# First-head copies on one queue, later beta gates and a layer norm in two streams, in a kernel whose order a list scheduler makes

## The chip, the cores and the metric

The kernel runs on one core of a Trainium2 chip. The metric is device time in microseconds (us) of one execution; each time of a kernel is a median of several runs; what is read from a trace (spans, waits, clock) is one profiled execution. Engines are named as the profile names them: PE is the matmul engine, PEld its weight load, DVE, ACT and POOL the vector, scalar and general engines, SP the sync engine, whose queue issues most DMAs. "SPq" and "ACTq" are those queues.

## The reference, cut

Two attention layers (32 heads of 20, four segments of 512 tokens with a compressive memory, a sigmoid gate on `beta`) alternate with two feed-forward layers (FFN), each behind a layer norm without parameters, on 2048 tokens of width 640:

```python
x = A_x
x = x + _A_ref(_layernorm(x), A_wq, A_wk, A_wv, A_wo, A_beta)
x = x + _B_ref(_layernorm(x), B_w1, B_w2)      # the "second layer norm" feeds this
x = x + _A_ref(_layernorm(x), A_wq, A_wk, A_wv, A_wo, A_beta)
x = x + _B_ref(_layernorm(x), B_w1, B_w2)
# in _A_ref, for segment s: softmax(q k^T * scale + mask) v, mixed by g = sigmoid(beta)
# with phi(q) M / (phi(q) z), where M and z sum phi(k) v and phi(k) of earlier segments
```

## The kernel before

The kernel is not written in the order in which it runs. Each piece of work is a Python generator, a *stream*, that yields operations with the tokens they wait for; a list scheduler with a small table of guessed costs picks, again and again, the operation that it believes can start first. The result is a fixed instruction order for each engine. So an edit to one stream may reorder the whole program.

```python
SWITCH_NS = 96.0      # the scheduler's guesses; none of them is emitted
COLS_LAG = 1500.0
SEM_NS = 60.0
...
# Sched.run: among the heads of all streams
key = (round(start + late), 0.5 if op.urgent else prio, self.rank[id(st[1])], n)
if best is None or key < best[0]:
    best = (key, st, end, start, k, op)
...
self.P.waits(e, waits)          # emit on engine e
self.free[e] = end              # the scheduler's belief of when e is free again
```

The scores of two head groups at once are made in five *rounds*. A round takes two score buffers. A third is lent during the first 20 rounds; after that there are only two, so the next round can't start before the exponentials of the last have emptied them. Matmuls come in three kinds: full (projections, FFN), row-tiled (scores, L1078), column-tiled (L1172 and the leftover FFN block, L1345).

```python
ROUNDS = (((0, 0, 0),), ((0, 1, 0), (0, 3, 384)), ((0, 2, 0), (1, 2, 256)),
          ((1, 0, 0),), ((1, 1, 0), (1, 3, 384)))
...
ready = sorted((s for s in SC if s.free), ...)
if len(ready) < 2 ...:          # a round takes two free score buffers
    return None, None
```

The four places that the change touches:

```python
# 1. beta gates, in consts(): when the stream may go on to the sigmoid of beta
tb = yield dma("sp", sem_("d_beta"), ...)
yield Need("stg", 0, 0, 0, 1)
te = yield act(32, lambda e: e.activation(gt[:, 0, :], beta_bc[:], ACT.Exp), [tb], psum=False)
# ... five small DVE operations, then omg and maskg

# 2. second layer norm: one stream that does both pairs of tiles in turn
def lnorm(s, x_tks, pool_, parts=1):
    n = 4 // parts
    for p0 in range(0, 4, n):
        ...   # stats of n tiles, rstd, then normalise and DMA-transpose pairs
def ln_b(a, s):
    xa = [[("xA", a, s, i, 0), ("xA", a, s, i, 1)] for i in range(NJ)]
    xt, xtk = yield from lnorm(s, xa, XNT_B, parts=2)
    S.set("hx", a, s, tks=[xt] + xtk)

# 3. proj_ln: the first norm of segment 3 is held back
if (a, s) == (0, 3):
    yield Need("sc",3,4,1)

# 4. first_heads: copies of the first q and k heads; z=0 by SP, z=1 by ACT
tk = yield dma(("sp", "act")[z], sem, 2048 * (rb - ra), ...,
               ev + sl.tks, issue=720.0, rate=200.0)
```

The softmax here doesn't subtract the row's maximum and nothing guards it: scores larger than these inputs give would overflow.

## Time and profile before

| | before |
|---|---|
| median of 4 runs | 570.1 us (568.55 to 570.87) |
| profiled span | 568.2 us |
| median that the prediction started from (3 of them) | 570.66 us |
| PE busy | 555.0 us, 98% |
| DVE, ACT busy | 409 us, 412 us |
| changes between kinds of matmul, from the instruction order | 394 |

PE is the bound. These are two lines of the page: PE's busy time with its share of the span and number of instructions, and the granted PE clock in 40 slices, in tenths.

```profile
PE 555.0 (98%) x5212; PEld 297.3 (52%) x5212; DVE 409.1 (72%) x1049; ACT 412.4 (73%) x527; POOL 192.1 (34%) x302
...
PEclk9999998999999999999999999999999999999999
```

A busy PE can hide slack, since matmuls overlap. I therefore also worked with the starts of the matmuls in the trace: between two of 320 columns lie 136 ns, between two of 512 columns 216 ns. The Trainium skill, "TensorEngine Tiling (Array Packing)", Key Properties, says that a change of tiling mode drains the engine; the trace agrees and gives the price, if from the step between two starts the streaming time of the first matmul is taken off: 96 ns from full to row-tiled, 91 to 101 ns back, 93 ns from full to column-tiled, 96 ns back.

The chain of waits, by engine, says the same: most of the span is PE's own work.

```profile
PE 80%; DVE 11%; DMA 5%; ACT 2%; SPq 1%; issue 1%; POOL 0%
```

From the starts of the matmuls I worked out *lost time*: for each pair of neighbouring matmuls, what their starts lie apart beyond the usual step for that pair of shapes (the 30th percentile in the kernel before, capped at 270 ns above streaming). Usual steps sum to 540.1 us before, lost time to 23.5 us (waits, half clock and all small delays).

The view of waits, limited to 89 to 103 us, says who waited for whom (us in total, times, longest):

```profile
PE ps L1345 <- DMA xnT<-xn_tok: 2.1, 1, 2.1
```

And the timeline of PE there (start, duration, operation, and in brackets the idle time before it):

```profile
92.19 0.72 PE L1172 MATMUL ps<-PT,v_aug 128*21 128x512 bf16 x16
92.91 0.40 PE L1078 MATMUL ps<-pad 20*128 20x384 bf16 x8
95.36 0.73 PE L1345 MATMUL ps<-xnT,w_r 128*32 128x256 bf16 x20 [2.05 <-DMA xnT<-xn_tok]
```

After the score round at 92.91 nothing was left but the leftover FFN block, and that waited for the transposed output of the second layer norm. In the trace's clock record a stretch at half clock follows, from 96.4 to 99.8 us.

### The profile page before, as it was taken

The page shows a single profiled execution, that of the slowest core. Times are in us where ns is not written, and L with a number is a line of the kernel's source. Part 1 is how long each engine was busy: PE and PEld are TensorE (multiplying, and loading weights), DVE is VectorE, ACT ScalarE, POOL GpSimd, SP SyncE. Part 2 cuts the span into 40 slices and gives each one's busy share as a digit, 9 for nine tenths or more (in the row PEclk, how much of TensorE's full clock was granted, in tenths as well). Part 3 has the DMA queues.
Part 4 walks back from the last instruction along what each step waited for, and adds up shares of the span by engine and source line. Part 5 has one row for each costly group of instructions (what it writes and reads, how often), then busy time and mean ns, then how long its engine had stood idle before and what let it go on. Part 6 is the DMA issues. An engine that isn't in the chain of part 4 may idle for free.

```text
span 568.2 us, 12813 instructions
## 1 busy us (share of the span) xinstructions
PE 555.0 (98%) x5212; PEld 297.3 (52%) x5212; DVE 409.1 (72%) x1049; ACT 412.4 (73%) x527; POOL 192.1 (34%) x302
## 2 busy tenths in 40 slices
PE   7999998999999999999999999999999999999998
PEld 6554553445554454655445545565545553665655
DVE  5957887888899888986688795599866875553202
ACT  5699878889879888887987687587876778313140
POOL 5336343333344343443334343044431433200000
PEclk9999998999999999999999999999999999999999
DMA  8685998735273415853377131771328420532101
GB/s 265 144 219 160 224 180 174 218 78 99 76 185 70 80 42 164 127 83 59 99 167 117 20 66 44 176 143 20 66 57 195 91 62 18 90 69 51 44 0 48
DMA packets 129980, 60.92 MB, mean 107 GB/s; under 512 B 108802, under 2 KB 119810, under 8 KB 129922
## 3 DMA queue, kind: packets, MB, share of 16 engines
q1 hardware_dynamic: 129504, 59.62, 47.4%
q8 instruction: 41, 0.67, 0.5%
q10 hardware_dynamic: 418, 0.49, 0.3%
q14 instruction: 17, 0.14, 0.1%
HBM read 20.57 MB, written 12.85 MB: 59 GB/s over the span
## 4 chain that ended last, share of the span: by engine, by line
PE 80%; DVE 11%; DMA 5%; ACT 2%; SPq 1%; issue 1%; POOL 0%
PE ps L601 52%; PE ps L598 11%; PE ps L1078 7%; PE ps L1172 5%; DMA otk<-otu 2%; PE ps L969 1%; DVE stats L609 1%; ACT PT L1140 1%; PE ps L1211 1%; DVE xn_tok L653 1%; PE ps L1021 1%; PE ps L1345 1%; DMA oT<-o_sb 1%; DVE otu L1182 1%; DMA pad<-scr 1%; DVE phs L936 1%
## 5 line engine op out<-in xcount | busy, mean ns | idle before, releaser
L1140 ACT ACTIVATE PT<-ps 128x1024 bf16<-128x1024 f32 x320 | 308.9, 1028 | 61.0 <-PE ps L1078 58.2
L1152 POOL TENSOR_SCALAR_AFFINE_SELECT PT<-PT 128x512 bf16<-128x512 bf16 x256 | 166.6, 668 | 271.7 <-ACT PT L1140 271.7
L601 PE MATMUL ps<-w_r,hT 128*128 128x320 bf16 x768 | 123.0, 299 | 0.0
L601 PE MATMUL ps<-xnT,w_r 128*128 128x512 bf16 x416 | 115.3, 383 | 0.0
L1294 DVE TENSOR_TENSOR x_sb<-x_sb,ps 128x320 bf16<-128x320 bf16 x128 | 60.6, 481 | 64.7 <-PE ps L601 63.7
L601 PEld LDWEIGHTS ps<-w_r,hT 128*128 128x128 bf16 x768 | 73.1, 98 | 32.3 <-issue 5.2
L1078 PE MATMUL ps<-pad 20*128 20x512 bf16 (+3 forms) x1024 | 63.6, 302 | 2.1 <-ACT PT L1140 1.0
L601 PEld LDWEIGHTS ps<-xnT,w_r 128*128 128x128 bf16 x416 | 39.5, 98 | 43.6 <-issue 4.8
L609 DVE BATCH_NORM_STATS2 stats<-x_sb 128x6 f32<-128x320 bf16 x124 | 55.2, 472 | 3.2 <-DMA x_sb<-in_A_x_dram 3.0
L1374 ACT ACTIVATE hT<-ps 128x512 bf16<-128x512 f32 x56 | 33.5, 599 | 22.2 <-PE ps L601 21.6
L601 PE MATMUL ps<-wo_r,oT 128*128 128x320 bf16 x256 | 46.8, 300 | 0.0
L1078 PEld LDWEIGHTS ps<-pad 20*128 20x128 bf16 x1024 | 17.9, 92 | 52.0 <-ACT PT L1140 24.7
L1182 DVE CAST otu<-ps 128x512 bf16<-128x512 f32 x47 | 32.3, 687 | 15.2 <-PE ps L1172 15.0
L1372 DVE TENSOR_SCALAR hT<-ps 128x512 bf16<-128x512 f32 x48 | 32.9, 685 | 12.3 <-PE ps L601 11.7
L1172 PE MATMUL ps<-PT,v_aug 128*21 128x128 bf16 (+3 forms) x896 | 40.5, 301 | 0.0
L598 PE MATMUL ps<-xnT,w_r 128*128 128x512 bf16 x104 | 39.9, 384 | 0.0
L625 POOL TENSOR_TENSOR rstd<-lnU,mhalf 128x2 f32<-128x2 f32 (+2 forms) x26 | 20.6, 791 | 47.2 <-DVE lnU L621 45.0
L601 PE MATMUL ps<-wv_r,xnT 128*128 128x320 bf16 x192 | 36.5, 299 | 0.0
L601 PE MATMUL ps<-xnT,wk_r 128*128 128x512 bf16 (+1 forms) x128 | 34.9, 366 | 0.0
L601 PE MATMUL ps<-xnT,wq_r 128*128 128x512 bf16 (+1 forms) x128 | 34.6, 366 | 0.0
L935 ACT ACTIVATE stg<-stg 128x512 bf16<-128x512 bf16 x50 | 31.6, 635 | 3.4 <-DVE rtmp L933 3.2
L653 DVE TENSOR_SCALAR xn_tok<-x_sb,mv,rstd 128x640 bf16<-128x640 bf16 x60 | 30.4, 536 | 3.9 <-POOL rstd L625 3.8
(108 smaller groups left out, 675.1 us busy)
## 6 DMA issues: line engine op xcount, KB each, us to landing
pad<-scr SPq DMA_DIRECT2D x124, 80.0 KB
scr<-stg SPq DMA_DIRECT2D x34, 256.0 KB, 2.7
out_dram<-x_sb SPq DMA_DIRECT2D x16, 160.0 KB, 1.8
w_r<-in_B_w_dram SPq DMA_DIRECT2D x10, 216.0 KB, 2.7
w_r<-in_B_w_dram SPq DMA_DIRECT2D x13, 160.0 KB, 2.7
x_sb<-in_A_x_dram SPq DMA_DIRECT2D x10, 160.0 KB, 3.0
scr<-w_r SPq DMA_DIRECT2D x5, 256.0 KB, 3.0
wv_r<-in_A_wv_dram SPq DMA_DIRECT2D x1, 800.0 KB, 9.3
```

Source lines behind the costliest of these rows:

```text
L598: bk, tk = yield pe(mm_ns(n), [(lambda e, bk, a=a, b=b: e.matmul(bk.ap[:, 0:n] if len(b.shape) == 2 else bk.ap[:, 0:n].rearrange("p (i n) ...
L601: tk = yield pe(mm_ns(n), [(lambda e, k=k, a=a, b=b, bk=bk: e.matmul(bk.ap[:, 0:n] if len(b.shape) == 2 else bk.ap[:, 0:n].rearrange("p (i ...
L609: tk = yield dve(320, 1, lambda e, c2=c2: e.bn_stats(stats6[:, t % 12, c2, :], x_sb[:, t, c2 * 320:(c2 + 1) * 320]), xt)
L653: nm = lambda e, bx, t, k: e.tensor_scalar(bx.ap[:, k * D:k * D + D], x_sb[:, t + k, :], mv[:, t + k, 0:1], rstd[:, t + k:t + k + 1], ALU. ...
L1078: fns.append([(lambda e, z=z, j=j, hh=hh, N=N, o=o, sl=sl, q=hh % 2: e.matmul(slot.ap[:, q, o:o + N], sl.ap[32 * hh:32 * hh + DH, z, 0, 12 ...
L1140: tx = yield act(1024, lambda e, dst=dst, src=src: e.activation(dst, src, ACT.Exp, scale=SCALE), sc + pw)
L1152: tm = yield pool(600.0, lambda e, reg=reg: e.affine_select(out=reg, in_=reg, pattern=[[0, 4], [1, 128]], compare_op=ALU.is_ge, fill=0.0, ...
L1172: fns.append((lambda e, OD, j=j, hh=hh: e.matmul(OD.ap[32 * hh:32 * hh + DH + 1, 128 * j:L], VAUG[vx(a, s)][:, j, 4 * g + hh, :], pt.ap[:, ...
L1182: te = yield evac(L, 1, lambda e: e.tensor_copy(dst, OD.ap), lambda e: e.activation(dst, OD.ap, ACT.Copy), [tk] + OTU[0].tks)
L1294: ta = yield dve(320, 1, lambda e: e.tensor_tensor(x_sb[:, t, 320 * hf:320 * hf + 320], x_sb[:, t, 320 * hf:320 * hf + 320], bk.ap[:, 0:32 ...
L1372: th = yield evac(512, 1, lambda e, dc=dc, bk=bk: e.tensor_scalar(hT[:, dc, :], bk.ap[:, :], 0.0, None, ALU.max), lambda e, dc=dc, bk=bk: ...
L1374: lambda e, dc=dc, bk=bk: e.activation(hT[:, dc, :], bk.ap[:, :], ACT.Relu), [tk] + HT.tks)
```

## The change

The intent as one reads it: let each half of the second norm go as soon as its tiles are ready, so that the wait just shown shrinks; free ACT's queue of DMA issues; take the wait for beta off the front of ACT.

```diff
-            yield Need("stg", 0, 0, 0, 1)
+            yield Need("ex", 0, 1)                       # beta gates
...
-        def lnorm(s, x_tks, pool_, parts=1):
+        def lnorm(s, x_tks, slot, p0=0, n=NJ, key=None):
...
-            if (a, s) == (0, 3):                          # norm of segment 3
-                yield Need("sc",3,4,1)
...
-                        tk = yield dma(("sp", "act")[z], sem, ...
+                        tk = yield dma("sp", sem, ...      # first heads
...
-        def ln_b(a, s):
-            xt, xtk = yield from lnorm(s, xa, XNT_B, parts=2)
-            S.set("hx", a, s, tks=[xt] + xtk)
+        def ln_b(p):
+            def f(a, s):
+                key = ("hslot", a, s)
+                slot = Acq(XNT_B) if p == 0 else Need(*key)
+                xt, xtk = yield from lnorm(s, xa, slot, 2 * p, 2, key)
+                S.set("hn", a, s, p, tks=xtk)
+                if p == 1:
+                    t0 = yield Need("hn", a, s, 0)
+                    S.set("hx", a, s, tks=[xt] + t0 + xtk)
+            return f
...
-        S.add(2, each(ln_b))
+        S.add(2, each(ln_b(0)))
+        S.add(2, each(ln_b(1)))
```

More of the change, by code (lines that the diff above doesn't have):

```diff
@@ L633, in turn @@
             return tk
-        def lnorm(s, x_tks, pool_, parts=1):
-            n = 4 // parts
+        def lnorm(s, x_tks, slot, p0=0, n=NJ, key=None):
             done = []
             xt = None
-            for p0 in range(0, 4, n):
+            if True:
                 aggr = []
@@ L649, in lnorm @@
                 if xt is None:
-                    xt = yield Acq(pool_)
+                    xt = yield slot
+                    xt = xt[0] if isinstance(xt, list) else xt
+                    if key is not None and p0 == 0:
+                        S.set(*key, tks=[xt])
                 for i in range(p0, p0 + n, 2):
@@ L744, in proj_ln @@
                 yield Need("sc",2,3,1)
-            if (a, s) == (0, 3):
-                yield Need("sc",3,4,1)
             early = a == 0 and s in (1, 2)
-            xt, xtk = yield from lnorm(s, xw, [XNT_E[s - 1]] if early else XNT_A)
+            xt, xtk = yield from lnorm(s, xw, Acq([XNT_E[s - 1]] if early else XNT_A))
             xt.users = []
@@ L885, in first_heads @@
                         p0 = 32 * hh + ra - r0
-                        tk = yield dma(("sp", "act")[z], sem, 2048 * (rb - ra), lambda e, p0=p0, ra=ra, rb=rb, c=c, z=z: e.dma_start(
+                        tk = yield dma("sp", sem, 2048 * (rb - ra), lambda e, p0=p0, ra=ra, rb=rb, c=c, z=z: e.dma_start(
                             sl.ap[p0:p0 + rb - ra, z], stg[ra - 128 * c:rb - 128 * c, c]), ev + sl.tks, issue=720.0, rate=200.0)
@@ L1326, in out_proj @@
             return f
-        def ln_b(a, s):
-            xa = [[("xA", a, s, i, 0), ("xA", a, s, i, 1)] for i in range(NJ)]
-            xt, xtk = yield from lnorm(s, xa, XNT_B, parts=2)
-            S.set("hx", a, s, tks=[xt] + xtk)
+        def ln_b(p):
+            def f(a, s):
+                xa = [[("xA", a, s, i, 0), ("xA", a, s, i, 1)] for i in range(NJ)]
+                key = ("hslot", a, s)
[6 more added lines that the diff above has]
+            return f
         HALF = {}
```

## The prediction

> **What bounds the kernel.** The median is 570.66 us, the profiled span 568.2 us. In the busy table PE has 555.0 us (98%), ACT 412, DVE 409, POOL 192. The chain of waits is 80% PE. Matmuls overlap, so busy PE can hide slack; their starts in the timeline don't: 136 ns apart for 320 columns and 216 ns for 512, nearly everywhere. Summing those steps over the 5212 matmuls (row- and column-tiled ones four abreast) gives about 505 us, my estimate of pure streaming. The rest is mostly changes between full, row-tiled and column-tiled matmuls, 0.1 to 0.26 us each in the timeline. The Trainium skill's "TensorEngine Tiling (Array Packing)", Key Properties, says a change of tiling mode drains the engine; the gaps agree.
>
> Real waits of PE are few: about 3.5 us before 10 us (first loads and norm), 0.5 at 21 us, 0.9 at 32 us (pad from scratch), 0.9 at 55 us, and the largest, 2.05 us at 93 us, where the first leftover FFN block waits for the second layer norm's transpose. A half-clock stretch follows, 96.4 to 99.8 us, costing up to 1.7 us (estimate: half of 3.4). Everything removable is about 8 us, 1.4%.
>
> **What the change does.** No arithmetic is added or removed, and the instruction order has 394 changes of tiling mode in both kernels. It is a rescheduling.
> 1. First heads: ACT's five issues (0.7 us each) go to the sync queue. ACT's 2.4 us gap at 15 us should shrink. The second head lands near 22.5 us (estimate); its first use is at 24 us. Near zero.
> 2. Beta gates leave the front of ACT and DVE and return later. Near zero.
> 3. Layer norm for segment 3 is no longer held back, and the second norm's halves have their own streams. Segment 1's projections move forward: the pause of the exponentials at 61 to 68 us disappears, and score rounds are a group of five ahead when the first leftover FFN block comes.
> 4. The cost: just before that block the new order has three successive score rounds with only 0.3 us of full matmuls among them. A round is gated by two exponentials of 0.97 us plus handovers, about 2.6 us. I estimate 8 us of rounds against 3.3 us of PE work, so the stall near 100 us grows from 2 to about 5 us, again followed by a half-clock stretch.
>
> So 2 to 3 us are gained early, about 3 us are lost at the first FFN, and the tail, dense FFN matmuls from about 475 us, is untouched. ACT's total is unchanged and bounds nothing.
>
> **Predicted:** 570.0 us, 564.5 to 575.5 at 8 in 10. Faster by over 2%: 0.02; within 2%: 0.95; slower: 0.03.
>
> **What would show each step.** Busy table: PE, ACT and DVE within 1% of before. Waits: PE's waits from 92 to 106 us total 4 to 6 us; those near 55 us shrink. Timeline: no 2.4 us gap of ACT at 15 us; no pause of the exponentials at 61 to 68 us; first scores still near 18 us. Granted clock: one half-rate stretch in mid-span.
>
> **What would make it wrong.** The small rounds overlap work I counted as serial, and the stall vanishes (then about 565). The fuller sync queue delays the scratch loads at 32 us, and each later round waits behind it. The reordering makes new waits in later segments, where today there are almost none.

## More of the kernel before

Where PE is short of work shows in this view of stretches: start and end, their length, then the busy time of each engine, PE's clock, the DMA share and GB/s.

```profile
core 0: us, PE busy (x) PEld busy (x) DVE busy (x) ACT busy (x) POOL busy (x), PEclk, DMA share, GB/s
15.00:50.00 35.00, 33.12 (x413) 17.88 (x411) 27.04 (x75) 29.52 (x38) 14.23 (x22) 1.00 0.72 178
50.00:75.00 25.00, 24.01 (x298) 13.53 (x295) 19.91 (x59) 21.74 (x30) 10.86 (x16) 1.00 0.88 211
75.00:90.00 15.00, 14.69 (x138) 7.17 (x137) 14.96 (x40) 13.09 (x18) 7.07 (x10) 1.00 0.76 141
90.00:106.00 16.00, 13.95 (x128) 5.35 (x127) 10.51 (x24) 12.67 (x18) 5.20 (x8) 0.89 0.85 181
106.00:300.00 194.00, 192.84 (x1864) 97.82 (x1863) 163.42 (x408) 166.12 (x204) 77.97 (x119) 1.00 0.51 110
```

In the stretch from 90 to 106 us PE is busy for 13.95 of 16 us, at a mean clock of 0.89.

## The result, and the profile after

The changed kernel took 573.68 us (median of 4, 573.09 to 573.99) against 570.1 us; the ratio is 1.0065, 95% interval 1.004 to 1.009. Ratios here compare the fast runs of the two kernels in the same rounds, so they are not quite the ratios of the medians, nor of the table's medians to 570.1.

Busy time and clock after:

```profile
PE 556.5 (97%) x5212; PEld 298.3 (52%) x5212; DVE 411.8 (72%) x1048; ACT 414.4 (72%) x528; POOL 192.2 (34%) x302
...
PEclk9999999899999999999999999999999999999999
```

The chain by engine has more of ACT in it (5%, before 2%), the first sign that exponentials now hold PE up:

```profile
PE 83%; ACT 5%; DMA 5%; DVE 5%; SPq 2%; issue 0%; POOL 0%
```

The matmuls are the same 5212. Usual steps sum to 540.4 us, nearly as before, lost time to 27.1 us: 3.6 us more, which is most of the 4.0 us between the spans. The stretches after, in the same columns:

```profile
15.00:50.00 35.00, 33.98 (x395) 18.16 (x393) 25.05 (x69) 30.07 (x40) 12.77 (x20) 1.00 0.75 183
50.00:75.00 25.00, 22.10 (x306) 11.88 (x303) 22.20 (x62) 23.55 (x29) 13.47 (x20) 1.00 0.94 202
75.00:90.00 15.00, 15.00 (x150) 7.87 (x147) 14.54 (x38) 13.18 (x18) 6.62 (x10) 1.00 0.82 164
90.00:106.00 16.00, 12.51 (x142) 4.99 (x134) 13.16 (x35) 13.51 (x16) 7.27 (x12) 0.79 0.74 181
106.00:300.00 194.00, 191.68 (x1808) 96.52 (x1804) 159.76 (x398) 156.99 (x191) 74.28 (x113) 1.00 0.47 101
```

Two of the short ones lost: from 50 to 75 us PE is busy for 22.10 us instead of 24.01, and from 90 to 106 us for 12.51 instead of 13.95, at a clock of 0.79 instead of 0.89. The waits behind the first loss, in the changed kernel and then in the kernel before, from 50 to 75 us:

```profile
PE ps L1078 <- ACT PT L1140: 1.2, 2, 0.9
PE ps L1021 <- DMA phk<-phs: 0.9, 1, 0.9
PE ps L1211 <- POOL PT L1152: 0.3, 1, 0.3
PE ps L598 <- DMA hT<-xn_tok: 0.2, 1, 0.2
```

```profile
PE ps L598 <- DVE w_r L786: 0.9, 1, 0.9
```

(The last stretch, 106 to 300 us, is also 1.2 us less busy, but it holds fewer matmuls, 1808 instead of 1864, since the changed kernel does them at another time.) The waits of PE from 92 to 106 us:

```profile
PE ps L1078 <- ACT PT L1140: 3.4, 2, 2.0
```

The releaser is no longer the norm's transpose but the exponentials. The timeline of PE shows why:

```profile
94.94 0.40 PE L1078 MATMUL ps<-pad 20*128 20x384 bf16 x8
95.26 0.72 PE L1172 MATMUL ps<-PT,v_aug 128*21 128x512 bf16 x16
97.36 0.40 PE L1078 MATMUL ps<-pad 20*128 20x256 bf16 x8 [1.38 <-ACT PT L1140]
99.79 0.61 PE L1078 MATMUL ps<-pad 20*128 20x512 bf16 x4 [2.03 <-ACT PT L1140]
100.49 1.25 PE L1172 MATMUL ps<-PT,v_aug 128*21 128x512 bf16 x16
101.67 0.81 PE L969 MATMUL ps<-BD,phs 128*128 128x147 bf16 x6
102.43 0.61 PE L1078 MATMUL ps<-pad 20*128 20x384 bf16 x8
102.98 1.26 PE L1352 MATMUL ps<-xnT,w_r 128*32 128x256 bf16 x20
```

Four score rounds (L1078) stand at 94.94, 97.36, 99.79 and 102.43 us. Between the first three PE has only one column-tiled group; between the last two a group and six short matmuls (L969). Each round waits until two exponentials of the one before it, about 0.97 us each, have freed its buffers; the first three rounds start 2.42 and 2.43 us apart. I call a round *empty* when PE has next to no full matmuls (under about 0.9 us of them) between it and the next round. From 100.49 on matmuls take longer than usual: the column-tiled group 1.25 us instead of 0.72. The clock record has half clock from 98.2 to 105.0 us, twice as long as before. The leftover FFN block (L1352) comes at 102.98 us, with no wait of its own.

### The profile page after: what moved, and what is told of

Same layout as the page of the kernel before. It is cut to its first block, busy times and chain, and to the rows that moved or that the text cites. A ratio compares the mean times of both kernels' runs of the same rounds, so it can differ in the third digit from the quotient of the medians.

```text
span 572.2 us, 12815 instructions
## 1 busy us (share of the span) xinstructions
PE 556.5 (97%) x5212; PEld 298.3 (52%) x5212; DVE 411.8 (72%) x1048; ACT 414.4 (72%) x528; POOL 192.2 (34%) x302
## 4 chain that ended last, share of the span: by engine, by line
PE 83%; ACT 5%; DMA 5%; DVE 5%; SPq 2%; issue 0%; POOL 0%
PE ps L601 54%; PE ps L598 11%; PE ps L1078 8%; PE ps L1172 6%; ACT PT L1140 5%; DMA phk<-phs 2%; PE ps L969 2%; PE ps L1021 1%; DMA pad<-scr 1%; PE ps L1352 1%; DMA oT<-o_sb 1%; DVE stats L609 1%; SPq L906 1%; DMA x_sb<-in_A_x_dram 1%; DVE x_sb L1294 1%; SPq L631 0%
## 5 line engine op out<-in xcount | busy, mean ns | idle before, releaser
L1078 PE MATMUL ps<-pad 20*128 20x512 bf16 (+3 forms) x1024 | 63.8, 303 | 5.4 <-ACT PT L1140 4.6
L1381 ACT ACTIVATE hT<-ps 128x512 bf16<-128x512 f32 x58 | 34.7, 598 | 22.0 <-PE ps L601 21.5
L1078 PEld LDWEIGHTS ps<-pad 20*128 20x128 bf16 x1024 | 17.9, 92 | 55.5 <-ACT PT L1140 29.8
L1379 DVE TENSOR_SCALAR hT<-ps 128x512 bf16<-128x512 f32 x46 | 31.4, 683 | 9.6 <-PE ps L601 9.5
L787 ACT ACTIVATE stg<-ps 128x512 bf16<-128x512 f32 (+1 forms) x44 | 24.4, 560 | 13.4 <-PE ps L601 13.1
L936 DVE TENSOR_TENSOR phs<-stg,rtmp 128x512 bf16<-128x512 bf16 x50 | 23.5, 471 | 13.2 <-ACT stg L935 12.3
```

The costliest lines, as they stand in the source:

```text
L1078: fns.append([(lambda e, z=z, j=j, hh=hh, N=N, o=o, sl=sl, q=hh % 2: e.matmul(slot.ap[:, q, o:o + N], sl.ap[32 * hh:32 * hh + DH, z, 0, 12 ...
L1379: th = yield evac(512, 1, lambda e, dc=dc, bk=bk: e.tensor_scalar(hT[:, dc, :], bk.ap[:, :], 0.0, None, ALU.max), lambda e, dc=dc, bk=bk: ...
L1381: lambda e, dc=dc, bk=bk: e.activation(hT[:, dc, :], bk.ap[:, :], ACT.Relu), [tk] + HT.tks)
```

## The experiments

The parts were tried alone and one by one removed, and the instruction order of each build was compared first, with buffers and waits. Two findings needed no chip. With the beta edit undone, or with the segment 3 edit undone, or both, the changed kernel's program is *identical* on all five engines: once the copies are on the sync queue, these two edits decide nothing. And the copies' move alone gives the same program as all edits but the split norm. So the changed kernel is two edits: the copies, and the split. The empty rounds are already in the order of the copies' move alone.

The theory, A: the move of the copies leads the scheduler to an order with empty rounds, and these, with the half clock behind them, cost the time. Rivals: B, the split norm costs it; C, nine copies in line on the sync queue delay what stands behind them; D, the loss is spread over many places.

This table holds the lost time of one profiled execution by PE's progress (its sum of usual steps; 45 us of it are reached near 51 us of the span, 75 near 85, 95 near 108). "Half clock" is what its clock record shows between 10 us and the last 10 us; it can differ from run to run of one kernel (see "The idle rounds filled").

| run | median us | ratio to before | lost to 45 | 45 to 75 | 75 to 95 | after 95 | half clock us |
|---|---|---|---|---|---|---|---|
| before | 570.1 | 1 | 6.1 | 1.3 | 5.0 | 11.2 | 3.4 |
| changed | 573.68 | 1.0065 | 4.9 | 4.2 | 7.0 | 11.1 | 6.8 |
| heads_only | 576.03 | 1.0122 | 5.7 | 3.5 | 8.9 | 11.2 | 10.2 |
| ln_only | 570.73 | 1.002 | 5.6 | 2.9 | 0.8 | 15.4 | 6.8 |
| before_order_sync_issue | 571.83 | 1.0045 | 8.4 | 2.9 | 4.5 | 11.5 | 10.2 |
| after_order_act_issue | 572.95 | 1.0065 | 5.0 | 3.8 | 7.6 | 9.7 | 6.8 |
| after_switch_100 | 568.66 | 0.999 | 4.6 | 4.5 | 1.1 | 11.0 | 0 |
| after_sem_62 | 573.08 | 1.0075 | 4.6 | 3.5 | 7.3 | 10.5 | 6.8 |
| beta_only | 566.99 | 0.996 | 5.5 | 3.4 | 1.2 | 11.6 | 0 |
| beta_and_ln | 571.67 | 1.0036 | 5.4 | 3.6 | 2.7 | 13.8 | 0 |
| gate_only | 569.62 | 1.0005 | 5.6 | 1.3 | 5.3 | 10.9 | 3.4 |
| before_sem_62 | 575.02 | 1.0099 | 5.6 | 3.6 | 7.6 | 13.4 | 10.2 |
| beta_cols_1400 | 569.84 | 1.0005 | 5.0 | 3.7 | 2.6 | 13.0 | 0 |

One more run, after_filled, has matmuls added and stands by itself below.

### The copies alone

```diff
-  tk = yield dma(("sp", "act")[z], sem, ...     # in the kernel before
+  tk = yield dma("sp", sem, ...
```

> The kernel before with only the first heads' five copies moved to the sync queue. Its instruction order has the same three score rounds with almost no full matmuls (0, 0 and 0.5 us) that the changed kernel has. Theory A (the order that the move of the copies brings about costs the time): 1.005 to 1.009 of before, and waits of the tensor engine of 4 to 6 us between 92 and 106 us. Theory B (the two-stream layer norm costs it): 0.998 to 1.002.

Measured: 576.03 us, ratio 1.0122 (1.0102 to 1.0143), slower than expected. The largest of PE's waits from 92 to 106 us is the changed kernel's (3.8 us in all, below the 4 to 6 us expected):

```profile
PE ps L1078 <- ACT PT L1140: 3.4, 2, 2.0
```

The half-clock stretch is 10.2 us long, three times that of before. So the copies' move brings the loss; on top of it the split norm, which is all that sets the changed kernel apart from this one, gives back about half of it (1.0122 to 1.0065, each against before in its own rounds).

### The split norm alone

The edits to `lnorm` and `ln_b` of the diff above, nothing else.

> The kernel before with only the second layer norm as two streams. Theory A: 0.996 to 1.003 of before, since no run of empty rounds is in its order. Theory B: 1.005 to 1.009. If the split does what it is meant to, the 2 us wait at 93 us is shorter.

Measured: 570.73 us, ratio 1.002 (0.9999 to 1.0041): Theory B, that the split costs the time, falls. The split does what it is meant to. PE's waits from 89 to 103 us, then from 106 to 125 us:

```profile
PE ps L1080 <- ACT PT L1142: 0.2, 1, 0.2
```

```profile
PE ps L1080 <- ACT PT L1142: 1.6, 1, 1.6
```

The 2.05 us wait at 93 us is gone, and by 108 us of before's span this run is 3.1 us ahead in lost time. Then a wait for exponentials at 117 us takes 1.6 us, with a half-clock stretch behind it, and the rest goes in small waits later. The gain is real where it was aimed and is given back in another place.

### Order or queue: two crossed kernels

Here the scheduler plans as in one kernel while the five copies are emitted to the other kernel's queue:

```diff
-            self.P.waits(e, waits)
+            q = getattr(op, "put", e)
+            self.P.waits(q, waits)
...
-                tk = self.P.dma(e, fns[0][0], op.dma)
+                tk = self.P.dma(q, fns[0][0], op.dma)
...
-                        tk = yield dma(..., issue=720.0, rate=200.0)
+                        op = dma(..., issue=720.0, rate=200.0)
+                        op.put = "sp"                    # before's order, sync queue
+                        # or ("sp", "act")[z]            # changed order, both queues
+                        tk = yield op
```

> Every engine keeps the order of the kernel before; only the five copies of the first heads are really issued by the sync queue instead of ACT's. Theory A (order): within 1 us of before, 0.998 to 1.002. Theory C (nine copies in line on the sync queue delay the scratch loads and with them the scores): 1.004 or more, with longer waits of the scores for the pads near 32 us. ACT's 2.4 us gap at 15 us should be gone in either.

> Every engine keeps the order of the changed kernel; only the five copies are issued by ACT's queue again. Theory A (order): within 1 us of the changed kernel, 1.005 to 1.008 of before, with the waits between 95 and 104 us still there. Theory C: back to 0.998 to 1.002.

In the changed order the queue makes no difference: 572.95 us and 1.0065, the changed kernel's ratio. This agrees with the Trainium skill, "DMA: Bandwidth & Descriptors", Issuing engines are not separate DMA queues, which says that several issuing engines save only the sequencer's time to issue.

In before's order it costs: 571.83 us, 1.0045 (1.0023 to 1.0066), against the expectation of Theory A. This is Theory C in the form given above, though not through the scratch loads that its expectation named: no wait for them is left near 32 us (0.93 us in before). What is delayed is the beta load. ACT's timeline in before (one line), then in this run:

```profile
19.28 0.23 ACT L563 ACTIVATE gt<-beta_bc 128x32 f32<-128x32 bf16 x1 [1.22 <-DMA beta_bc<-in_A_beta_dram]
```

```profile
17.45 0.60 ACT L788 ACTIVATE stg<-ps 128x512 bf16<-128x512 f32 x1 [2.00 <-PE ps L602]
21.05 0.23 ACT L564 ACTIVATE gt<-beta_bc 128x32 f32<-128x32 bf16 x1 [3.00 <-DMA beta_bc<-in_A_beta_dram]
21.18 1.00 ACT L1143 ACTIVATE PT<-ps 128x1024 bf16<-128x1024 f32 x1
```

The beta load stands behind six copies on the sync queue instead of four and is issued at 18.39 us instead of 16.43. ACT, which works in order, waits 3.00 us for it (1.2 us in before) with the first exponentials standing behind, and PE then waits 1.9 us for these instead of 0.5. So the beta edit looks like the companion of the copies' move, but before's order with both was not run. (The profiled execution is the slowest of this kernel's six, 573.83 us, with more half clock than the others had, so its 10.2 us in the table is not typical.) In the changed kernel the scheduler knew the load was late and had put the gates back by itself, hence the edit without effect. ACT's 2 us of idleness at 15 us are there even without its issues (2.00 us before the operation at 17.45): it waited for a matmul group, not for its queue.

### The same edits, without the empty rounds

```diff
-SWITCH_NS = 96.0          # in the changed kernel; a guess of the scheduler
+SWITCH_NS = 100.0
```

```diff
-SEM_NS = 60.0             # in the changed kernel
+SEM_NS = 62.0
```

> The changed kernel with one number of the scheduler's own cost table altered (its guess of a mode change, 96 to 100 ns), which changes nothing but the order, from the 102nd row of the tensor engine on. No round with under 0.9 us of full matmuls is left ahead of the first leftover FFN block. Theory A (order, the empty rounds): waits between 92 and 106 us fall under 2 us, and the time falls by 3 to 5 us, to 0.998 to 1.002 of before. Rival D (the changed kernel loses time spread over many places, the empty rounds are only where it shows): 1.004 or more.

> The changed kernel with another number of the same table altered (handover, 60 to 62 ns). Its order is the changed kernel's through row 380 of the tensor engine, so the three empty rounds stay, and differs only later. Theory A: 1.004 to 1.010 of before. It also tells how much a different order after 130 us is worth: I expect 1.5 us at most.

The first has all the edits of the change but no empty round: 568.66 us, ratio 0.999 (0.9972 to 1.0008). Its waits of PE from 89 to 106 us and the stretch from 90 to 106 us:

```profile
PE ps L1078 <- ACT PT L1140: 0.2, 1, 0.2
```

```profile
90.00:106.00 16.00, 15.82 (x156) 6.99 (x155) 15.72 (x44) 14.16 (x19) 6.66 (x10) 1.00 0.97 208
```

PE is busy for 15.82 of 16 us at full clock. The second keeps the changed order past 104 us, empty rounds included, and differs only later: 573.08 us, 1.0075 (1.0052 to 1.0097). Two builds of the same edits, about 4.4 us apart, and of their lost time 6.2 us apart between 75 and 95 us of progress. Between these two builds Rival D, that the loss is spread out, falls.

Against before the account is less simple. Of the lost time that the changed kernel has more than before, 2.0 us stand between 75 and 95 us of progress, where the empty rounds are, but 2.9 us between 45 and 75, and 1.2 us were gained earlier. after_switch_100 pays the middle part as well (4.5 us) and makes it up where it has no empty rounds (1.1 us instead of before's 5.0). Theory A is thus shown for the stretch of the empty rounds; what costs the 2.9 us ahead of it was not tested.

### Empty rounds without any of the edits

```diff
-SEM_NS = 60.0             # in the kernel before
+SEM_NS = 62.0
```

> The kernel before, none of the four edits made, with the scheduler's handover guess set to 62 ns: a new order with two empty rounds ahead of the first leftover FFN block (before has none ahead of it). Theory A says the empty rounds cost whatever brought them about: 3 us or more of waits at 88 to 100 us, 1.002 to 1.006 of before. If empty rounds as such cost nothing, 0.998 to 1.001.

Measured: 575.02 us, 1.0099 (1.0067 to 1.0132), slower than expected. PE's timeline has the two empty rounds, at 94.37 and 96.91 us (the next round comes at 100.64):

```profile
94.37 0.40 PE L1078 MATMUL ps<-pad 20*128 20x384 bf16 x8
96.91 0.40 PE L1078 MATMUL ps<-pad 20*128 20x512 bf16 x4 [2.14 <-ACT PT L1140]
98.38 0.93 PE L1172 MATMUL ps<-PT,v_aug 128*21 128x512 bf16 x8 [1.08 <-POOL PT L1152]
```

Empty rounds cost here too, 7.6 us lost between 75 and 95 instead of 5.0. This build also has a 2.1 us wait at 54.5 us and more lost later than before has, so not all of its 1% is theirs. It is also a warning: a guess altered by 2 ns, and no work at all, moves this kernel by 1%.

### The idle rounds filled

```diff
+        def keep_warm():
+            for m, u, n in ((6, 1, 14), (6, 2, 26)):
+                t = yield Need("sc", m, u, 1)
+                bk, tk = yield pe(26.0, [(... e.matmul(bk.ap[:, 0:128], ident[:], ident[:], ...), k == n - 1)
+                                         for k in range(n)], t[1:], acq=MISC, mode="rows")
+                bk.release(tk)
...
+        S.add(1, keep_warm())         # in the changed kernel
```

> The changed kernel with 14 and 26 matmuls of the identity, whose results nobody reads, in the two long waits at 96 and 98 us; the order is otherwise the changed kernel's up to the first leftover FFN block, and differs a little after it. Theory A1 (the half clock after the waits comes from the idleness): no half-clock stretch near 98 to 105 us, and 1 to 2 us faster than the changed kernel. If the clock falls to half all the same, the idleness is not its cause. The waits for the exponentials are as long in either case, only filled.

The fillers and the rounds they stand between, on PE:

```profile
97.31 0.96 PE L591 MATMUL ps<-ident 128*128 128x128 bf16 x14
98.75 0.40 PE L1087 MATMUL ps<-pad 20*128 20x256 bf16 x8 [0.49 <-ACT PT L1149]
99.25 1.62 PE L591 MATMUL ps<-ident 128*128 128x128 bf16 x26
101.18 0.39 PE L1087 MATMUL ps<-pad 20*128 20x512 bf16 x4 [0.30 <-ACT PT L1149]
```

The clock record has no half-clock stretch left in this execution, and all four runs show a granted clock of 1.0 (the changed kernel's four: 0.994), so the idleness brings it about. The waits for exponentials shrink to 0.49 and 0.30 us because 0.96 and 1.62 us of useless matmuls stand in them.

From the round at 94.94 us to the sixth after it, at 111.13 us, the changed kernel takes 16.19 us; here it is 15.51 us, from 96.33 to 111.84 us. These 0.7 us are not the price of the half clock, since the work in the two stretches differs: the changed kernel's has the leftover FFN block and 16 full matmuls of 512 columns after the block, the filled one's has no block and 22. Over the first three rounds, where the useful work is the same, it is 7.49 against 7.28 us. The starts of the changed kernel's matmuls in its half-clock stretch add up to 2.6 us more than the usual steps (1.6 us in before's stretch); how much of that would have been waiting anyway is not known.

The recorded runs give another measure. Of the 33 runs of the kernel before that were made beside the experiments, 12 show a granted clock of 1.0 and 19 of 0.997 (one stretch of 3.4 us at half clock lowers the mean by 0.003), and their mean times are 568.56 and 569.66 us. So a stretch goes with about 1.1 us, though a run may be slower for the wait that brings the stretch as well.

The filled kernel as a whole was slower, 575.99 us (1.0118), where 1 to 2 us less than the changed kernel had been expected; the order after the FFN block differs and has new waits of up to 1.2 us between 188 and 205 us; as a version it is no use.

### The other edits alone, and tries at a faster version

```diff
-            yield Need("stg", 0, 0, 0, 1)      # beta_only, in the kernel before
+            yield Need("ex", 0, 1)
```

> The kernel before with only the beta gates moved behind the first score rounds (copies still split over two queues). In the changed kernel this edit alters no instruction, but alone it gives another order, without empty rounds, with the pause of the score rounds shortened. ACT no longer waits 1.2 us for beta ahead of the first exponential. Theory A: 0.994 to 1.000 of before.

Measured: 566.99 us (566.78 to 567.39), ratio 0.996 (0.9946 to 0.9974). The stretch from 90 to 106 us:

```profile
90.00:106.00 16.00, 15.81 (x156) 6.81 (x155) 12.84 (x38) 14.58 (x19) 6.67 (x10) 1.00 0.83 230
```

There is no empty round, no half clock, and 1.2 us lost between 75 and 95 us of progress where before has 5.0. It is the one version that is faster than the kernel before beyond the noise, by a little.

> The changed kernel with only the move of the five copies undone (they stay on two queues). Theory A: the move of the copies is what brings the empty rounds, so without it the stall near 97 us is gone and the time is 0.994 to 1.000 of before, about that of the beta edit alone. If the two-stream norm or the beta edit were to blame, it would stay at 1.004 or more.

The copies' move undone in the changed kernel: 571.67 us, 1.0036 (1.001 to 1.0061). This missed its expectation. The part that Theory A speaks of came true (2.7 us lost between 75 and 95, no half clock), but 13.8 us are lost later, against 11.2 in before, in waits of 0.7 to 0.9 us at 192, 241, 251 and 363 us among others. Theory A tells the loss of one stretch, not the total.

> The kernel before with only the layer norm of segment 3 no longer held back. In the changed kernel this edit alters no instruction; alone its order parts from before's at row 160 of the tensor engine, with one empty round ahead of the first leftover FFN block. Theory A: about like before, 0.998 to 1.004, with 2 to 3 us of waits at 88 to 98 us.

Segment 3's norm not held back, in the kernel before: 569.62 us, 1.0005, within its expectation, with the wait for exponentials at 92.5 us that its one empty round foretold.

> A try at a version faster than both: the beta edit alone, with another of the scheduler's guesses altered (the lag for column-tiled matmuls, 1500 to 1400), whose order has no empty round from the 20th round on. Theory A: 0.993 to 0.999 of before.

`COLS_LAG` at 1400 with the beta edit: 569.84 us, 1.0005 (0.9974 to 1.0035). Missed: 2.6 us lost between 75 and 95, but 13.0 later. An order without empty rounds does not by itself make a good time.

## Why the prediction was right or wrong

The range (564.5 to 575.5) and the class (within 2%) held. The central figure, 570.0, was 3.7 us too low: a gain of 2 to 3 us and a loss of about 3 were to cancel, and both terms came out as losses. That the range held says little of the mechanism, since it was 11 us wide and all builds of the table but one (heads_only) fall in it, whatever their edits. Point by point:

- **"Everything removable is about 8 us", PE bound, the tail untouched.** Not put to the test: no build came more than 3.1 us below before (566.99 against 570.1 us). That PE stays the bound held: its busy time differs from before's by 0.3%, DVE's by 0.7%, ACT's by 0.5% in the changed kernel.
- **The stall grows from 2 to about 5 us, followed by a half-clock stretch.** The mechanism was right: three successive score rounds, gated by exponentials, at the place named. A round takes 2.42 to 2.43 us where nothing else holds it, not 2.6. Its size was somewhat off: the two listed waits total 3.4 us, below the 4 to 6 us that I named as the sign, but the half clock lasts 6.8 us, not one stretch of 3.4. In lost time this stretch costs 7.0 us instead of 5.0, so 2.0 more, where I had said about 3.
- **"2 to 3 us are gained early" is the step that failed.** By 51 us the changed order is 1.2 us ahead. Then, up to 85 us, it loses 2.9 us more than before. The pause of the exponentials at 61 to 68 us did go, and the wait of 0.9 us at 55 us with it, but waits of 0.2 to 0.9 us between 58 and 70 us took their place, for exponentials, for the causal mask on POOL, for a norm's transpose and for the transposed phi(k). The term of the sum measured a loss of 1.7 us, not a gain of 2 to 3. Before and gate_only, which keep the pause and have no half clock there, lose 1.3 us between 45 and 75 of progress; all other runs lose 2.9 to 4.5. Why an order without the pause, or with a shorter one, loses more there was not tested.
- **"First heads: near zero."** True for the queue on the chip, in the changed order (crossed kernel: 0.7 us and the same ratio). As an input to the scheduler the move of five copies is the origin of the new order. I gave the reordering to the segment 3 edit and to the split norm; the builds show that the segment 3 and beta edits alter no instruction there. Nor did I see that in before's order the move would have cost about 2.5 us (ratio 1.0045), with the beta load as the wait that the trace shows.
- **ACT's gap of 2.4 us at 15 us** did shrink (0.67 us at most), but not because the issues left: the crossed kernel has no issues on ACT and still 2.00 us. First scores came at 18.3 us, near 18 as said.

What stays open is the part after 95 us of progress: from order to order it varies from 9.7 to 15.4 us with no cause that these runs tell apart.

## What to carry to other kernels

When a scheduler makes the order, compare the built programs first: it shows without a chip which edits of a change do anything, and a neutral change of one guess shows how far the time moves for nothing. Then read what the scheduler puts between two links of a gated chain: each score round needed about 2.4 us of exponentials and handover, so other matmuls must last from one to the next. And when a wait goes away, look for where the chain closes up next; here the split norm removed a 2 us wait at 93 us, and a new one of 1.6 us stood at 117 us.

## What the Trainium skill lacked or had wrong

- "TensorE: Matmul & The Clock Gate", Why this matters for your kernels, advises no PE idle gaps over about 3 us. Here a single wait of 2.05 us (before, at 93 us) and one of 0.95 us (the split norm alone, at 54.5 us) were followed by half clock, while one of 0.94 us at 55.1 us in before was not. What sets the last two apart stays open. In the split norm alone the wait lies within one interval of the grid of the next point, in before it lies across an edge at 55.5 us; but the changed kernel's wait of 0.86 us before 58.79 us lies within one interval too, and no half clock follows.
- The same page, What's actually happening, gives a window of 3413 ns. The runs agree: half clock came in stretches of 3.41, 6.83 and 10.24 us, and within one trace the stretches start whole multiples of 3.413 us apart (24.5, 58.6 and 99.6 us in before_order_sync_issue: 10 and 12 of them). What such a stretch costs in this kernel was not isolated: about 1.1 us goes with one of 3.4 us in the runs of the kernel before.
- "TensorEngine Tiling (Array Packing)", Key Properties, says that a mode change drains the engine but gives no price. Measured, beyond the streaming of the matmul before: 96 ns from full to row-tiled, 91 to 101 ns back, 93 ns from full to column-tiled, 96 ns back; the kernel before has 394 changes.
- "DMA: Bandwidth & Descriptors", Issuing engines are not separate DMA queues, is right about bandwidth, but a reader may miss that the place in a queue matters: with five more copies on the sync queue, two of them ahead of the small beta load, ACT waited 3.00 us for it instead of 1.2.
